# Weights stored as float64: two VectorE instructions a piece to make float32, instead of three

## The chip, the core and the metric

The kernel runs on one core of one Trainium2 chip. A core has five engines with a queue of instructions each: TensorE (PE: matmuls and weight loads), VectorE (DVE), ScalarE (ACT), GpSimd (POOL) and SyncE (SP), which here issues all DMA transfers. Every engine takes its own instructions strictly in order and waits at semaphores for the others. The metric is the device time of one execution in microseconds (us).

## The reference

Local and global attention (8 batches, 8 heads, 512 local and 32 global positions, head size 64), then a two-layer network over all 4352 tokens.

```python
def reference(**kwargs):
    ...
    attn_out = _attn_ref(**attn_kwargs)        # softmax over a window of +-32 keys and 32 global keys
    B, H, S, D = attn_out.shape
    x = np.ascontiguousarray(attn_out.transpose(0, 2, 1, 3)).reshape(B * S, H * D)
    return _moe_ref(x=x, **moe_kwargs)

def _moe_ref(x, w_in, w_out):
    h = x @ w_in                               # (tokens, 512) @ (512, 2048)
    g = h * (1.0 / (1.0 + np.exp(-h)))
    return (g @ w_out).astype(np.float32)      # (tokens, 2048) @ (2048, 512)
```

The two weight matrices arrive as float64 (the draw is divided by a float64 square root), all else as float32.

## The kernel before

Every product is made of float32r parts: a value is cast to `hi`, and `lo` is the value minus `hi`; three matmuls (hi hi, hi lo, lo hi) are added in PSUM.

**Attention** is a stream of steps, each one 128 queries of two heads. A step k loads `raw` and `vraw`, splits them (`qk`, `klo`, `vhi`, `vlo`), makes scores `s` on TensorE, softmax in `probs` on VectorE and ScalarE, copies them by a DMA to `rr`, transposes them to `t`, splits that into `pt_hi` (ScalarE) and `pt_lo` (VectorE, L397), and multiplies with the values into `o`, which goes to `xh` and `xl` (L427, L428). GpSimd makes `klo` and `vlo` of the first 28 to 32 steps and the columns of `pt_hi` and `pt_lo` for the global queries (L404, L405).

**The two layers** run over blocks of 3 or 2 token tiles of 128. For each of 16 slices f of the hidden dimension, `first_layer` makes `h` (L550, 12 matmuls) and from it `gh` and `gl` (ScalarE L556 and L559, VectorE L557 and L560); `second_layer` adds that slice's product into `out` (L569 to L571). During a block, attention for the next block is put between the matmuls. Block 0 needs 12 steps of attention before it starts.

**The weights** are converted once, before and during block 0, in `load_weights`: 36 pieces, 28 of 512 columns and the last 8 of 256. SyncE loads a piece's 64-bit words into `raw_w` (three buffers for the pieces of 512, in turn). ScalarE reads the upper words as float32 and scales them by 2^-112 into `w` (L231), which puts the exponent where float32 wants it, but three bits too low. Three VectorE instructions mend that: L233 shifts by 3 into `raw_w`'s upper words, L234 joins this with the sign, L236 takes the three missing bits from the lower word. ScalarE casts `w` to `w_hi` (L238), and GpSimd subtracts for `w_lo` (L239). After that the buffers of `w` and `raw_w` are free again. First-layer slice f of block 0 needs the two or four pieces of slice f.

**The order.** TensorE's instructions stand in the order of the program text. On the other engines and on SyncE's queue a scheduler places the instructions when the kernel is built, from the waits among them and from its own estimate of durations, so a change in one instruction moves others.

Of the kernel before, what the change touches and what calls it, by code (L numbers as in the profile page):

```python
# [9 lines left out]
F32 = mybir.dt.float32  # L10
# [3 lines left out]
U32 = mybir.dt.uint32  # L14
AF = mybir.ActivationFunctionType
ALU = mybir.AluOpType
# [3 lines left out]
B, H, SL, SG, D = 8, 8, 512, 32, 64  # L20
P = 128
NC = SL // P              # query chunks of a sequence
NPR = H // 2              # pairs of heads, each one 128-row slice of the model dimension
NST = NC * NPR            # steps of a batch: a chunk for a pair of heads
W = 224                   # keys that a chunk of local queries sees: 192 local ones and the 32 global ones
# [8 lines left out]
NEG = -8.0e9              # times the scale of 1/8: -1e9  # L34
SCALE = 0.125

# [1 line left out]
SIZES = [3, 2] + [3] * 9 + [2]       # token tiles in each block of the two layers  # L38
NLATE = 4                            # slices of the weights that take the place of the first buffers
# [10 lines left out]
AHEAD = 12                           # steps before the first block is complete  # L50
# when the parts of a step are due, in steps' times after its scores
DUE = dict(load=-1.3, split=-0.4, vload=-0.4, vsplit=0.9, turn=1.45, out=2.15)
LAG = 1.0                            # more for the parts after the scores in the first steps
# [5 lines left out]
PRE, PACE, LOOK = 0, 0.75, 1         # weights converted during the first steps  # L59
END = 0.6                            # how far the attention is ahead of a block  # L60

DUE = dict(load=-1.2, split=-0.5, vload=-0.6, vsplit=0.95, turn=1.6, out=2.2)
LAG = 2.25
# [6 lines left out]
PACE = 0.85  # L70
PRE = 5
LOOK = 3
END = 0.5
# [14 lines left out]
SIZES = (3, 3, 3, 3, 3, 3, 3, 3, 3, 2, 3, 2)  # L88
# [5 lines left out]
def attention_moe_kernel(ctx: ExitStack, tc: tile.TileContext, qk0_in, qk_in, v_in, gqk, wts, out):  # L94
    nc = tc.nc
# [3 lines left out]
    work = ctx.enter_context(tc.tile_pool(name="work", bufs=1))  # L99
    two = ctx.enter_context(tc.tile_pool(name="two", bufs=2))  # L100
    small = ctx.enter_context(tc.tile_pool(name="small", bufs=4))
    # buffers of the first steps, in two parts that later hold the last slices of the weights
    first = [tc.tile_pool(name=f"first{i}", bufs=1, side=side) for i, side in enumerate(("left", "right"))]
# [5 lines left out]
    # until the layers start, attention has their banks too  # L109
    early, banks = [1], {"s": itertools.count(), "t": itertools.count(), "o": itertools.count()}  # L110
# [32 lines left out]
    # probabilities: columns past the window stay zero  # L143
# [6 lines left out]
    # transposed probabilities by unit and key tile; 32 more columns for the global queries  # L150
    # what of the first buffers is still in use
# [47 lines left out]
    def load_weights():  # L199
# [19 lines left out]
        if first[1]:  # L219
            raw = first_pool[1].tile([P, 2 * DM], I32, tag="raw", bufs=3, name=f"raw_w{f}_{c0}")  # L220
            w = first_pool[1].tile([P, n], F32, tag="w", bufs=2, name=f"w{f}_{c0}")
# [4 lines left out]
        if W0 <= 2 * f + c0 // DM < PIN:  # L226
            tc.keep_in_program_order(load)
        # float64 to float32: the upper word read as float32 and scaled by 2**-112 has the exponent
        # rebased three bits too low, below the sign; the lower word gives the last three bits
        words = raw.rearrange("p (n w) -> p n w", w=2)  # L230
        nc.scalar.activation(w, words[:, :, 1].bitcast(F32), AF.Copy, scale=2.0**-112)  # L231
        wi, up, low = w.bitcast(U32), words[:, :, 1].bitcast(U32), words[:, :, 0].bitcast(U32)
        nc.vector.tensor_scalar(out=up, in0=wi, scalar1=3, scalar2=None, op0=ALU.logical_shift_left)  # L233
        nc.vector.scalar_tensor_tensor(out=wi, in0=wi, scalar=0x80000000, in1=up, op0=ALU.bitwise_and,  # L234
                                       op1=ALU.bitwise_or)
        nc.vector.scalar_tensor_tensor(out=wi, in0=low, scalar=29, in1=wi, op0=ALU.logical_shift_right,  # L236
# [36 lines left out]
    # program order is the order of the data  # L273
# [43 lines left out]
    tiles = {}  # L317
# [37 lines left out]
    def st_scores(k, b, c, pr):  # L355
        qk, klo = tiles.pop(("qk", k))
        free(k)
        s = attbank("s", f"s{k}")
# [24 lines left out]
        # a copy that keeps every bit for the transpose  # L383
# [141 lines left out]
    outs, now = {}, [0, 0]  # L525

    def fill(part):
        """Attention for the next block, in step with this one."""
        now[1] += part
        n = now[0]  # L530
        total = NF * SIZES[n] + (NF - 1) * SIZES[n] + (SIZES[n - 1] if n else 0)
        if n + 1 < len(SIZES):
            advance(ends[n] + (ends[n + 1] - ends[n]) * min(1.0, now[1] / total / FULL))
# [7 lines left out]
    def first_layer(n, f):  # L541
# [13 lines left out]
        # twice h * sigmoid(h); the half goes into the way out  # L555
# [46 lines left out]
def _layout(q_l, k_l, v_l, q_g, k_g, v_g, w_in, w_out):  # L602
# [26 lines left out]
    # the first steps: both heads' keys once, and each one's queries zero on the other's rows  # L629
# [9 lines left out]
    # two heads on the rows; each one's queries are zero on the other's rows  # L639
# [28 lines left out]
```

## Time and profile before

| | |
|---|---|
| three executions | 1107.52, 1108.76 (median), 1111.5 us |
| span of the profiled execution | 1108.1 us (0.7 under the median; its own time is not recorded apart) |
| PE busy | 1042.5 us, 94% |
| DVE busy | 798.5 us, 72%, 2467 instructions |
| ACT busy | 725.1 us, 65% |
| POOL busy | 228.5 us, 21% |
| weight conversions (first L231 to last L239) | 17.4 to 202 us |
| TensorE clock granted, mean | 0.972 |

A share of busy time is a mean over stages: TensorE is full from about 220 us on, and before that it waits for the others. So a change in the conversions is to be read from the stage before 220 us alone. In the rows of the profile, `out<-in` are the names of the program without their numbers, `xN` is a count, and `<-` with an engine and a line names what ended an idle time.

### The profile page before, as it was taken

Reading aid. Unit: us, or ns where it says so; the run is one execution under the profiler, and the core shown is the slowest. Engines: PE = TensorE matmul, PEld = TensorE weight load, DVE = VectorE, ACT = ScalarE, POOL = GpSimd, SP = SyncE. Lnnn points to the kernel's source line nnn. Section 1 sums busy time; section 2 is a strip of 40 time slices with the busy share of each in tenths; the row PEclk is TensorE's granted clock in tenths of the full one; section 3 lists DMA queues with packets and bytes.
Section 4 is the critical chain, followed back from the end, with each engine's and each line's share of the span. In section 5 each row is a group of like instructions: output and inputs, shape, how many; then the busy total and the mean of one; then the engine's idle time right before and its main releaser. Section 6 shows DMA issues by size and latency. Waiting matters only on the chain.

```text
span 1108.1 us, 21579 instructions
## 1 busy us (share of the span) xinstructions
PE 1042.5 (94%) x6824; PEld 947.8 (86%) x6824; DVE 798.5 (72%) x2467; ACT 725.1 (65%) x1933; POOL 228.5 (21%) x441
## 2 busy tenths in 40 slices
PE   5647889999999999999999999999999999999998
PEld 4646778898999999999989999999999999889996
DVE  6989998777778867766667877777777768863322
ACT  7876676776677766766567776667666658763232
POOL 8756775321100111001010111101100011100000
PEclk8678899999999999999999999999999999999999
DMA  8576554543343443342233443334333324420000
GB/s 249 179 219 188 182 170 130 156 121 117 109 145 115 138 138 110 113 148 83 82 112 112 147 130 117 111 116 158 109 109 120 111 92 148 138 76 20 1 30 19
DMA packets 74800, 134.76 MB, mean 122 GB/s; under 512 B 10432, under 2 KB 30400, under 8 KB 74688
## 3 DMA queue, kind: packets, MB, share of 16 engines
q1 hardware_dynamic: 74688, 133.40, 38.8%
q8 instruction: 54, 0.88, 0.3%
q14 instruction: 58, 0.48, 0.1%
HBM read 86.44 MB, written 8.91 MB: 86 GB/s over the span
## 4 chain that ended last, share of the span: by engine, by line
PE 80%; DVE 10%; DMA 3%; issue 3%; ACT 3%; POOL 1%; SPq 0%; DVEq 0%; ACTq 0%; POOLq 0%
PE h L550 31%; PE out L569 11%; PE out L571 10%; PE out L570 10%; PE o L421 8%; PE s L369 4%; PE t L393 3%; DVE w L234 2%; DVE w L236 1%; DMA rr<-probs 1%; DMA raw_w<-in_wts_dram 1%; DVE raw_w L233 1%; DVE pt_lo L397 1%; ACT probs L377 1%; DVE probs L373 1%
## 5 line engine op out<-in xcount | busy, mean ns | idle before, releaser
L550 PE MATMUL h<-xh,w_hi 128*128 128x384 f32 (+1 forms) x768 | 255.6, 333 | 0.1
L550 PE MATMUL h<-xh,w_lo 128*128 128x384 f32 (+1 forms) x768 | 252.3, 329 | 0.0
L550 PE MATMUL h<-xl,w_hi 128*128 128x384 f32 (+1 forms) x768 | 252.1, 328 | 0.0
L569 PE MATMUL out<-w_hi,gh 128*128 128x512 f32 x544 | 224.8, 413 | 0.0
L571 PE MATMUL out<-w_hi,gl 128*128 128x512 f32 x544 | 215.6, 396 | 3.0 <-DVE gl L560 1.8
L570 PE MATMUL out<-w_lo,gh 128*128 128x512 f32 x544 | 214.7, 395 | 0.0
L556 ACT ACTIVATE t<-h 128x384 f32<-128x384 f32 (+1 forms) x192 | 90.5, 471 | 186.2 <-PE h L550 175.8
L404 POOL CAST pt_hi<-pgt 128x64 fp32r<-128x64 f32 (+1 forms) x160 | 50.4, 327 | 726.1 <-PE o L421 719.2
L557 DVE SCALAR_TENSOR_TENSOR t<-t,h 128x384 f32<-128x384 f32 (+1 forms) x192 | 101.6, 529 | 122.7 <-ACT t L556 121.7
L550 PEld LDWEIGHTS h<-xh,w_hi 128*128 128x128 f32 x768 | 145.4, 189 | 6.0 <-ACT xh L427 0.6
L550 PEld LDWEIGHTS h<-xl,w_hi 128*128 128x128 f32 x768 | 145.5, 189 | 5.4
L550 PEld LDWEIGHTS h<-xh,w_lo 128*128 128x128 f32 x768 | 145.3, 189 | 0.0
L560 DVE TENSOR_TENSOR gl<-t,gh 128x384 fp32r<-128x384 f32 (+1 forms) x192 | 107.3, 559 | 48.5 <-PE out L571 43.1
L571 PEld LDWEIGHTS out<-w_hi,gl 128*128 128x128 f32 x544 | 102.8, 189 | 28.4 <-DVE gl L560 4.6
L377 ACT ACTIVATE probs<-probs,st 128x224 f32<-128x224 f32 x256 | 121.4, 475 | 7.3 <-DVE st L373 6.2
L373 DVE CUSTOM_DVE_ANT_0 probs<-s,mask 128x224 f32<-128x224 f32 x256 | 89.3, 384 | 50.4 <-PE s L369 47.0
L421 PE MATMUL o<-pt_hi,vhi 128*64 128x160 f32 (+1 forms) x512 | 99.4, 238 | 20.1 <-ACT pt_hi L396 7.8
L570 PEld LDWEIGHTS out<-w_lo,gh 128*128 128x128 f32 x544 | 103.6, 190 | 11.2
L569 PEld LDWEIGHTS out<-w_hi,gh 128*128 128x128 f32 x544 | 103.2, 190 | 11.4 <-ACT gh L559 0.4
L559 ACT CAST gh<-t 128x384 fp32r<-128x384 f32 (+1 forms) x192 | 94.6, 493 | 21.2 <-DVE t L557 17.8
L421 PE MATMUL o<-pt_hi,vlo 128*64 128x160 f32 (+1 forms) x512 | 96.3, 237 | 0.0
L421 PE MATMUL o<-pt_lo,vhi 128*64 128x160 f32 (+1 forms) x512 | 79.8, 238 | 16.3 <-DVE pt_lo L397 11.8
(82 smaller groups left out, 2016.5 us busy)
## 6 DMA issues: line engine op xcount, KB each, us to landing
raw<-in_qk_dram SPq DMA_DIRECT2D x100, 352.0 KB, 3.0
rr<-probs SPq DMA_DIRECT2D x128, 256.0 KB, 2.3
vraw<-in_v_dram SPq DMA_DIRECT2D x128, 128.0 KB, 2.4
raw_w<-in_wts_dram SPq DMA_DIRECT2D x28, 512.0 KB, 4.0
raw_g<-in_gqk_dram SPq DMA_DIRECT2D x32, 304.0 KB, 2.8
out_dram<-o SPq DMA_DIRECT2D x32, 256.0 KB, 2.6
raw<-in_qk_dram SPq DMA_DIRECT2D x28, 240.0 KB, 3.6
rg<-pg SPq DMA_DIRECT2D x16, 256.0 KB, 2.4
```

What stands on the lines that cost most here:

```text
L373: nc.vector.tensor_tensor_reduce(out=p[:, u, :W], in0=s[:, u * W : (u + 1) * W], in1=mask_of[c], scale=-SCALE, scalar=3.0e38, op0=ALU.add, ...
L377: nc.scalar.activation(p[:, u, :W], p[:, u, :W], AF.Exp, bias=st[:, u : u + 1], scale=-1.0, accum_out=st[:, 2 + u : 3 + u])
L404: nc.gpsimd.tensor_copy(out=pt_hi[:n, :, a, P:], in_=g)
L421: nc.tensor.matmul(o[:D, u * wide : u * wide + m], v[:, a, u, :], pt[:, u, a, :m], start=(i == 0), stop=(i == len(terms) - 1))
L550: nc.tensor.matmul(h[:, :nt], wt, x[:, c, :nt], start=(i == 0), stop=(i == 3 * NCC - 1))
L556: nc.scalar.activation(t[:, :nt], h[:, :nt], AF.Tanh, scale=0.5)
L557: nc.vector.scalar_tensor_tensor(out=t[:, :nt], in0=t[:, :nt], scalar=1.0, in1=h[:, :nt], op0=ALU.add, op1=ALU.mult)
L559: nc.scalar.copy(out=gh[:, :nt], in_=t[:, :nt])
L560: nc.vector.tensor_tensor(out=gl[:, :nt], in0=t[:, :nt], in1=gh[:, :nt].bitcast(F32), op=ALU.subtract)
L569: nc.tensor.matmul(o, gh[:, sl], wh, start=(f == 0), stop=False)
L570: nc.tensor.matmul(o, gh[:, sl], wl, start=False, stop=False)
L571: nc.tensor.matmul(o, gl[:, sl], wh, start=False, stop=(f == NF - 1))
```

## The change

ScalarE's scaling becomes a leaky rectifier: `out = x` for a positive `x` and `-2^32 x` for a negative one, with x the scaled word. The result is never negative; a negative weight's exponent is greater by 32, which is a set bit at the place that becomes the sign after a shift by 3. The instruction that joined the sign apart goes. The shift for the lower word is made in place, in the lower words of `raw_w`, and needs only the loaded piece; the one join that is left shifts `w` by 3 and adds the three bits.

```diff
         words = raw.rearrange("p (n w) -> p n w", w=2)
-        nc.scalar.activation(w, words[:, :, 1].bitcast(F32), AF.Copy, scale=2.0**-112)
-        wi, up, low = w.bitcast(U32), words[:, :, 1].bitcast(U32), words[:, :, 0].bitcast(U32)
-        nc.vector.tensor_scalar(out=up, in0=wi, scalar1=3, scalar2=None, op0=ALU.logical_shift_left)
-        nc.vector.scalar_tensor_tensor(out=wi, in0=wi, scalar=0x80000000, in1=up, op0=ALU.bitwise_and,
-                                       op1=ALU.bitwise_or)
-        nc.vector.scalar_tensor_tensor(out=wi, in0=low, scalar=29, in1=wi, op0=ALU.logical_shift_right,
+        nc.scalar.activation(w, words[:, :, 1].bitcast(F32), AF.Prelu, scale=2.0**-112, alpha=-(2.0**32))
+        wi, low = w.bitcast(U32), words[:, :, 0].bitcast(U32)
+        nc.vector.tensor_scalar(out=low, in0=low, scalar1=29, scalar2=None, op0=ALU.logical_shift_right)
+        nc.vector.scalar_tensor_tensor(out=wi, in0=wi, scalar=3, in1=low, op0=ALU.logical_shift_left,
                                        op1=ALU.bitwise_or)
         nc.scalar.copy(out=hi, in_=w)
```

In the new kernel the rectifier is L233 on ScalarE, the shift L235 and the join L236 on VectorE; all other lines keep their numbers.

The scheduler's order moves with it. On VectorE, ahead of the `gl` of slice 1 in block 0 (`gl0_1`), these rows stand before, from the last joins of piece `w5_512` on (in a name like `w6_0` the 6 is the slice and the 0 the first column; the last number only tells buffers apart):

```order
L234 SCALAR_TENSOR_TENSOR w5_512_1371<-w5_512_1371,raw_w5_512_1370 128x512
L285 TENSOR_REDUCE gst1_1_1208<-pg1_125 128x1
L236 SCALAR_TENSOR_TENSOR w5_512_1371<-raw_w5_512_1370,w5_512_1371 128x512
L557 SCALAR_TENSOR_TENSOR t0_1_1185<-t0_1_1185,h0_1_1172 128x384
L286 TENSOR_SCALAR gst1_1_1208<-gst1_1_1208 128x1
L233 TENSOR_SCALAR raw_w6_0_1457<-w6_0_1458 128x512
L428 TENSOR_TENSOR xl_1_1216<-o12_1217,xh_1_1215 64x128
L435 TENSOR_TENSOR acc_130<-o12_1217,acc_130 64x32
L234 SCALAR_TENSOR_TENSOR w6_0_1458<-w6_0_1458,raw_w6_0_1457 128x512
L560 TENSOR_TENSOR gl0_1_1187<-t0_1_1185,gh0_1_1186 128x384
```

And now, ahead of the same `gl0_1`:

```order
L557 SCALAR_TENSOR_TENSOR t0_1_1177<-t0_1_1177,h0_1_1164 128x384
L235 TENSOR_SCALAR raw_w7_512_1560<-raw_w7_512_1560 128x512
L236 SCALAR_TENSOR_TENSOR w7_0_1553<-w7_0_1553,raw_w7_0_1552 128x512
L285 TENSOR_REDUCE gst1_1_1200<-pg1_125 128x1
L286 TENSOR_SCALAR gst1_1_1200<-gst1_1_1200 128x1
L235 TENSOR_SCALAR raw_w8_0_1654<-raw_w8_0_1654 128x512
L236 SCALAR_TENSOR_TENSOR w7_512_1561<-w7_512_1561,raw_w7_512_1560 128x512
L235 TENSOR_SCALAR raw_w8_512_1662<-raw_w8_512_1662 128x512
L288 TENSOR_SCALAR gst1_1_1200<-gst1_1_1200 128x1
L428 TENSOR_TENSOR xl_1_1208<-o12_1209,xh_1_1207 64x128
L435 TENSOR_TENSOR acc_130<-o12_1209,acc_130 64x32
L560 TENSOR_TENSOR gl0_1_1179<-t0_1_1177,gh0_1_1178 128x384
```

Pieces finished ahead of `gl0_1` are 12 before (through `w5_512`) and 16 now (through `w7_512`), and the next shifts stand ahead of the joins.

On SyncE's queue of transfers, from the copy of step 13's probabilities (`rr13`) on, the rows before are:

```order
L385 DMA rr13_1112<-probs1_122 128x512
L225 DMA raw_w6_512_1466<-in_wts_dram 128x1024
L225 DMA raw_w7_0_1566<-in_wts_dram 128x1024
L322 DMA raw19_1730<-in_qk0_dram 128x480
L329 DMA vraw16_1428<-in_v_dram 128x256
L225 DMA raw_w7_512_1575<-in_wts_dram 128x1024
L322 DMA raw20_1840<-in_qk0_dram 128x480
```

And now:

```order
L385 DMA rr13_1106<-probs1_122 128x512
L322 DMA raw18_1598<-in_qk0_dram 128x480
L225 DMA raw_w7_512_1560<-in_wts_dram 128x1024
L225 DMA raw_w8_0_1654<-in_wts_dram 128x1024
L225 DMA raw_w8_512_1662<-in_wts_dram 128x1024
L322 DMA raw19_1712<-in_qk0_dram 128x480
L225 DMA raw_w9_0_1766<-in_wts_dram 128x1024
```

Loads of weights have moved ahead of the steps' loads: `raw_w8_512` stands in front of `raw19` where before `raw_w7_0` did. ScalarE and GpSimd move in the same way, and TensorE not at all. ScalarE has one table load in both orders, as its second row.

## The prediction

> **What bounds the kernel now.** I read the page's slices first, to see where the matrix engine is not full.
>
> ```profile
> PE   5647889999999999999999999999999999999998
> ...
> DVE  6989998777778867766667877777777768863322
> ACT  7876676776677766766567776667666658763232
> POOL 8756775321100111001010111101100011100000
> ```
>
> A slice is 27.7 us. From the ninth slice on, TensorE is full nearly to the end; only the first 220 us can be shortened by work on another engine. All the weight conversions lie there. So I asked for the busy time of each engine by stage.
>
> ```profile
> core 0: us, PE busy (x) PEld busy (x) DVE busy (x) ACT busy (x) POOL busy (x), PEclk, DMA share, GB/s
> 20.00:80.00 60.00, 37.55 (x269) 34.24 (x268) 51.36 (x157) 47.24 (x133) 43.06 (x56) 0.70 0.69 215
> 80.00:140.00 60.00, 45.04 (x260) 39.34 (x258) 57.92 (x125) 41.43 (x104) 37.05 (x42) 0.89 0.59 182
> ...
> 143.80:160.00 16.20, 14.37 (x83) 12.83 (x82) 15.83 (x35) 11.62 (x28) 13.74 (x13) 0.89 0.61 183
> ...
> 160.00:200.00 40.00, 36.55 (x251) 32.76 (x250) 34.45 (x105) 28.36 (x80) 21.26 (x28) 1.00 0.45 131
> 200.00:220.00 20.00, 18.37 (x106) 16.39 (x105) 14.72 (x44) 15.19 (x40) 7.68 (x10) 0.91 0.59 169
> ```
>
> Between 80 and 140 us VectorE works 57.92 of 60 us (97%), while TensorE idles 15.0 us, ScalarE 18.6 and GpSimd 23.0: VectorE is the bound there. Before 80 us it works 86%, with the DMA engines at 0.69 and ScalarE at 79%: a mixture. After 160 us TensorE is at 91% and takes over. The chain of waits from 60 to 205 us says the same by line.
>
> ```profile
> by line: DVE w L234 14.8%; issue 12.7%; DVE w L236 8.9%; DMA raw_w<-in_wts_dram 8.2%; DVE raw_w L233 5.9%; PE h L550 4.4%; ACT probs L377 4.1%; DVE pt_lo L397 3.2%; PE o L421 3.2%; DVE gl L560 2.9%; PE s L369 2.6%; PE out L569 2.3%; DVE t L
> ```
>
> The three instructions that join the words of a weight piece (L233, L234, L236) make 29.6% of it. Their groups, shape by shape (busy us, mean ns of one):
>
> ```profile
> L234 DVE SCALAR_TENSOR_TENSOR w<-w,raw_w 128x512 uint32<-128x512 uint32 x28 | 30.3, 1083 | 0.6
> L236 DVE SCALAR_TENSOR_TENSOR w<-raw_w,w 128x512 uint32<-128x512 uint32 x28 | 25.7, 917 | 0.3
> L233 DVE TENSOR_SCALAR raw_w<-w 128x512 uint32<-128x512 uint32 x28 | 18.0, 642 | 6.1 <-ACT w L231 6.1
> L234 DVE SCALAR_TENSOR_TENSOR w<-w,raw_w 128x256 uint32<-128x256 uint32 x8 | 4.0, 504 | 0.4
> ```
>
> These means are far above what the same instructions take alone. The fastest, median and slowest of each, and two places in order of time:
>
> ```profile
> L233 DVE TENSOR_SCALAR raw_w<-w x36: 280/418/1443, 18.1 to 199.1; 128x512 uint32<-128x512 uint32 x28, 128x256 uint32<-128x256 uint32 x8
> L234 DVE SCALAR_TENSOR_TENSOR w<-w,raw_w x36: 424/693/1777, 18.6 to 199.5; 128x512 uint32<-128x512 uint32 x28, 128x256 uint32<-128x256 uint32 x8
> L557 DVE SCALAR_TENSOR_TENSOR t<-t,h x7: 527/542/544, 92.9 to 140.1; 128x384 f32<-128x384 f32 x7
> ...
> 72.21 0.69 DVE L234 SCALAR_TENSOR_TENSOR w<-w,raw_w 128x512 uint32<-128x512 uint32 x1
> ...
> 85.35 1.28 POOL L239 TENSOR_TENSOR w_lo<-w,w_hi 128x512 fp32r<-128x512 f32 x1
> 85.41 1.78 DVE L234 SCALAR_TENSOR_TENSOR w<-w,raw_w 128x512 uint32<-128x512 uint32 x1
> ```
>
> The join at 72.21 took 0.69 us with GpSimd idle; the same one at 85.41 began just after a GpSimd subtraction of 1.28 us, took 1.78, and ended 0.56 after that subtraction. L557, which reads one operand from PSUM, never stretches (527 to 544). So the bare prices are 0.42 us for a shift and 0.69 for a join, and the rest of the means is waiting for GpSimd.
>
> **The change, part by part.** *One VectorE join less.* A 512-column piece now takes one shift and one join. Bare, it falls from 0.42 + 2 x 0.69 = 1.80 us to 1.11; with today's waits from 0.642 + 1.083 + 0.917 = 2.64 to 0.642 + 1.000 = 1.64 (1.000 is the mean of the two joins). Over the 36 pieces L234 holds 30.3 + 4.0 = 34.3 us. That is not the gain: the run shortens only where VectorE ends last, and the order of work moves too.
>
> *Conversions move ahead.* TensorE's order is unchanged; on VectorE, ScalarE, GpSimd and the load queue the pieces of weights now stand earlier among the attention work. I counted, in the two orders, the finished pieces ahead of a result that TensorE needs: ahead of the gl of slice 2 they are 14 before and 18 now, of slice 6, 21 and 28, ahead of step 18's pt_lo, 25 and 28. Slice 6's gl is the tightest. In the trace it is the seventh L560:
>
> ```profile
> 143.78 1.57 DVE L560 TENSOR_TENSOR gl<-t,gh 128x384 fp32r<-128x384 f32 x1
> ```
>
> VectorE's conversion work ahead of it was 21 x 1.80 = 37.8 us and is now 28 x 1.11 = 31.1, bare: 6.7 less. With today's waits it is 21 x 2.64 = 55.4 and 28 x 1.64 = 45.9: 9.5 less. I take the middle, -8.1. (Step 18's pt_lo gains 25 x 1.80 - 31.1 = 13.9 and so does not bind.) The early stage, where VectorE is not alone, is inside this number; that its share is fully collected is assumed.
>
> The Trainium skill (SBUF — State Buffer, section "Who interferes with whom") says that a VectorE instruction with two SBUF inputs and a GpSimd instruction that reads SBUF share one read interface, which whoever is first holds for its whole instruction while the other is blocked. The pair at 85.35 and 85.41 agrees. By that rule the wait is a remainder of GpSimd's work, which stays, and the next two-input instruction meets it: the term would be -6.7, not -8.1, and the sum 1.4 us later.
>
> *What follows slice 6.* From 143.8 to 220 us TensorE idles 1.83 + 3.45 + 1.63 = 6.9 us. With VectorE nearly rid of conversions by then, some of that goes; other waits (block change, attention's own chain) stay. Half: -3.4, ends 0 and -6.9.
>
> *New waits for weights.* Pieces come closer together, while the buffers of raw words stay three. A load cannot be issued before the join three pieces back is done, and the next shift needs its landing.
>
> ```profile
> raw_w<-in_wts_dram SPq DMA_DIRECT2D x17, 512.0 KB, 3.9
> SPq L225 <- DVE w L236: 24.0, 8, 4.6
> ```
>
> The first row (80 to 160 us) gives 3.9 us from issue to landing; the second says that loads already wait for the join. Where the pieces stand densest (front of slice 1's gl) VectorE has some 2.5 to 3.5 us of bare work between a join and the shift that needs that buffer again, so it stands still for about a microsecond at each of a few pieces, with attention's pieces queued behind it and TensorE behind those. +2, ends 0 and +5. On the load queue, steps' own loads and the copies of probabilities stand behind the same loads; that is inside these ends.
>
> *The shift* used to wait for ScalarE (6.1 us of idle in its row) and now waits for the load alone: free, hidden or given to the term above. It now reads every second word and writes it back; no row shows both. L233 writes every second word at 0.42, the joins read them at 0.69. I take 0.42, from the row with the same kind of instruction; at 0.69 the 28 pieces would lose 28 x 0.27 = 7.6 us.
>
> *The rectifier* on ScalarE instead of a copy with a scale: operands are the same immediates and one table load stands in both orders. No row shows a rectifier.
>
> ```profile
> L231 ACT ACTIVATE w<-raw_w 128x512 f32<-128x512 f32 x28 | 18.7, 667 | 5.9 <-DMA raw_w<-in_wts_dram 3.2 <-POOL w_lo L239 2.6
> L238 ACT CAST w_hi<-w 128x512 fp32r<-128x512 f32 x28 | 17.3, 618 | 10.0 <-DVE w L236 9.9
> L287 ACT ACTIVATE pg<-pg,gst 128x544 f32<-128x544 f32 x16 | 12.0, 750 | 8.6 <-DVE gst L286 8.3 <-DVE acc L435 0.3
> ```
>
> Between the plain cast (618) and an exponential with a per-row operand (750) it costs -0.05 to +0.08 a piece, -1.4 to +2.2 us over 28; ScalarE's 18.6 idle us between 80 and 140 cover it, and without that cover it is those ends. I take 0.
>
> **Sum.** -8.1 - 3.4 + 2 = -9.5, made against the span of 1108.1: 1098.6. The median of the runs, 1108.76, stands 0.7 above that span, so 1099. The ends of the terms: -9.5 - 6.9 + 0 = -16.4, 1092; and -6.7 + 0 + 5 = -1.7, 1107, the edge of no change. About 0.3% (3.3 us) is what a measurement of this kernel can tell from nothing.
>
> **The rivals.** *The waits go with the instruction.* If fewer two-input instructions meet GpSimd, the remaining ones may run bare: 55.4 - 31.1 = 24.3 us ahead of slice 6, with 6.9 after it 31, or 1078. For it: L234 alone carries 28 x (1.083 - 0.693) = 10.9 us of waiting. Against: GpSimd's subtractions stay as many, and TensorE's 15.0 idle us between 80 and 140 are nearly all there is to win. Typically 1085; range 1078 to 1092.
>
> *Nothing arrives.* The shift at 0.69 takes the -8.1 to about -0.5, or the waits for loads do it; with the tail of -3.4 and +2 the result is 1107. For it: transfers already run at 182 GB/s in that stage and the loads wait for buffers. Against: the trace shows no VectorE wait on a weight load above the ones ahead of L233.
>
> *Slower: ScalarE becomes the bound.* The seven pieces moved ahead of slice 6 bring ScalarE 7 x (0.667 + 0.618) = 9.0 us more in front of it, and nothing is taken off ScalarE. If it ends last, what is won on VectorE doesn't count: 9.0 - 3.4 = +5.6, or 1114. This decides once more than 18.6 - 9.0 = 9.6 of ScalarE's idle us between 80 and 140 cannot be filled. These are its waits from 80 to 160:
>
> ```profile
> ACT w_hi L238 <- DVE w L236: 7.9, 7, 2.3
> ACT probs L381 <- DVE st L380: 3.6, 4, 1.5
> ACT t L556 <- DVE gl L560: 2.7, 3, 1.0
> ACT xh L427 <- PE o L421: 2.5, 2, 1.3
> ```
>
> Most are waits for VectorE, which shrink with its load: against the rival. GpSimd, whose subtractions move ahead in the same way, has 23.0 idle us and is further off. That the rectifier is not what runs (a second table load, say) is included here with 1 in 100.
>
> **How the numbers follow.** The forecast case (1092 to 1105.4) 0.56; waits gone 0.17; nothing arrives (1105.4 to 1112) 0.15; slower 0.12. The predicted time is the first's, 1099, its own range 1092 to 1105. To leave out no more than 2 in 10 the range runs to 1086 (half of the second case) and 1110 (past the third and into the fourth). Faster by over 0.3%: 0.56 + 0.17 = 0.73; within: 0.15; slower: 0.12.
>
> **What would show it.** The join at L236, 36 times, bare 0.69; the shift at L235 with a median near 0.42 and no wait for ScalarE; L233 on ScalarE near 0.67 with a single table load. VectorE's busy time about 25 to 34 us less, and below 90% between 80 and 130 us. TensorE full from some 10 us earlier. Shifts that wait for raw_w transfers, a few us in all. I am wrong if the shift's median is 0.69, if ScalarE's share rises over 90% in that stage, or if waits for weight loads exceed 5 us.

## The result, and the profile after

The changed kernel takes 1115.98 us (median; 1113.88 to 1117.41), the kernel before 1108.39 beside it: a ratio of 1.0061, 95% interval [1.0042, 1.0080], 0.6% slower. The forecast was 1099.0 with a range of 1086 to 1110. The profiled execution took 1115.36 us, its span 1113.5.

The page's totals and its slices, in the order in which the prediction read them:

```profile
PE 1049.1 (94%) x6824; PEld 954.9 (86%) x6824; DVE 780.6 (70%) x2431; ACT 725.9 (65%) x1933; POOL 220.3 (20%) x441
...
PE   4667797999999999999999999999999999999998
...
DVE  5888887667777876876667877778767667873322
```

VectorE has 36 instructions and 17.9 us of work less (798.5 before), and slices two, four, five and six show it: 8 where 9 stood. TensorE isn't full any earlier: its first slices read 4667797, before 5647889. Busy time by stage:

```profile
20.00:80.00 60.00, 38.53 (x263) 34.93 (x262) 46.80 (x149) 48.45 (x133) 40.44 (x57) 0.64 0.70 223
80.00:140.00 60.00, 46.40 (x246) 40.74 (x246) 52.57 (x114) 43.05 (x107) 39.61 (x43) 0.80 0.65 207
140.00:160.00 20.00, 18.03 (x114) 16.39 (x113) 17.28 (x36) 13.34 (x34) 12.87 (x14) 0.91 0.27 81
160.00:200.00 40.00, 33.48 (x211) 29.54 (x210) 27.94 (x82) 25.43 (x73) 15.20 (x23) 0.91 0.43 128
200.00:220.00 20.00, 20.00 (x139) 18.66 (x137) 12.21 (x42) 14.61 (x40) 8.85 (x13) 1.00 0.42 121
```

Between 80 and 140 us VectorE works 52.57 of 60 us, no longer 57.92. It is no longer full, yet TensorE gets through 246 matmuls there, fewer than the 260 before. The instructions themselves (groups by shape, busy us, mean ns, idle before; then fastest/median/slowest):

```profile
L236 DVE SCALAR_TENSOR_TENSOR w<-w,raw_w 128x512 uint32<-128x512 uint32 x28 | 27.2, 975 | 1.5 <-ACT w L233 1.3
L235 DVE TENSOR_SCALAR raw_w<-raw_w 128x512 uint32<-128x512 uint32 x28 | 21.0, 749 | 8.7 <-DMA raw_w<-in_wts_dram 8.7
L233 ACT ACTIVATE w<-raw_w 128x512 f32<-128x512 f32 x28 | 18.7, 671 | 0.9 <-DMA raw_w<-in_wts_dram 0.7
...
L235 DVE TENSOR_SCALAR raw_w<-raw_w x36: 292/430/1703, 18.0 to 198.0; 128x512 uint32<-128x512 uint32 x28, 128x256 uint32<-128x256 uint32 x8
L236 DVE SCALAR_TENSOR_TENSOR w<-w,raw_w x36: 418/688/2026, 19.1 to 200.4; 128x512 uint32<-128x512 uint32 x28, 128x256 uint32<-128x256 uint32 x8
```

The bare prices are as forecast: shift 0.43 us, join 0.69, rectifier 0.67. The means lie above them where GpSimd works at the same time: of the 28 large joins the seven that overlap no GpSimd work took 0.68 to 0.69 us and the others up to 2.03. The shift, which reads one operand only, is stretched in the same way: 0.40 to 0.43 us without such work, up to 1.70 with it. The waits and the chain (20 to 220, and 60 to 205 us):

```profile
DVE raw_w L235 <- DMA raw_w<-in_wts_dram: 13.7, 13, 2.0
ACT w L233 <- DMA raw_w<-in_wts_dram: 7.9, 7, 1.9
...
by line: DMA raw_w<-in_wts_dram 23.7%; issue 8.0%; DVE w L236 7.5%; PE h L550 7.4%; DVE raw_w L235 7.3%; PE s L369 4.1%; PE out L569 3.9%; PE out L570 3.4%; PE out L571 3.3%; PE o L421 3.1%; DVE gl L560 2.5%; DVE pt_lo L397 2.2%; DMA raw_g<
```

Transfers of weights have gone from 8.2% of that chain to 23.7%, and VectorE waits 13.7 us for them. That looks like the culprit; the experiments say that it is a small part. Two milestones, step 11's `pt_lo` and slice 6's `gl`:

```profile
83.52 0.68 DVE L397 TENSOR_TENSOR pt_lo<-t,pt_hi 128x512 fp32r<-128x512 f32 x1
...
151.02 0.59 DVE L560 TENSOR_TENSOR gl<-t,gh 128x384 fp32r<-128x384 f32 x1
```

Step 11 is where it was (83.19 before), so nothing of the lighter conversion arrived by then. Slice 6's `gl` is 7.2 us later (143.78), and the span 5.4 us longer. Piece `w12_512` meanwhile is joined at 142.18 us, before at 162.47: the weights come early and the layers late.

### The profile page after: what moved, and what is told of

Same layout as the page of the kernel before. It is cut to its first block, busy times and chain, and to the rows that moved or that the text cites. A ratio compares the mean times of both kernels' runs of the same rounds, so it can differ in the third digit from the quotient of the medians.

```text
span 1113.5 us, 21495 instructions
## 1 busy us (share of the span) xinstructions
PE 1049.1 (94%) x6824; PEld 954.9 (86%) x6824; DVE 780.6 (70%) x2431; ACT 725.9 (65%) x1933; POOL 220.3 (20%) x441
## 4 chain that ended last, share of the span: by engine, by line
PE 82%; DVE 7%; DMA 6%; issue 2%; ACT 2%; SPq 0%; POOL 0%; ACTq 0%; DVEq 0%; POOLq 0%
PE h L550 32%; PE out L569 11%; PE out L571 10%; PE out L570 10%; PE o L421 8%; PE s L369 5%; DMA raw_w<-in_wts_dram 4%; PE t L393 3%; DMA rr<-probs 1%; DVE raw_w L235 1%; DVE w L236 1%; DVE probs L373 1%; DVE pt_lo L397 1%; DMA raw_g<-in_gqk_dram 1%; PE gs L268 1%
## 5 line engine op out<-in xcount | busy, mean ns | idle before, releaser
L550 PE MATMUL h<-xh,w_hi 128*128 128x384 f32 (+1 forms) x768 | 256.5, 334 | 0.0
L550 PE MATMUL h<-xl,w_hi 128*128 128x384 f32 (+1 forms) x768 | 253.5, 330 | 2.1 <-DVE xl L428 2.1
L550 PE MATMUL h<-xh,w_lo 128*128 128x384 f32 (+1 forms) x768 | 253.9, 331 | 0.0
L550 PEld LDWEIGHTS h<-xl,w_hi 128*128 128x128 f32 x768 | 146.3, 191 | 8.0 <-DVE xl L428 2.6
L550 PEld LDWEIGHTS h<-xh,w_hi 128*128 128x128 f32 x768 | 146.2, 190 | 5.4
L550 PEld LDWEIGHTS h<-xh,w_lo 128*128 128x128 f32 x768 | 146.2, 190 | 0.0
L560 DVE TENSOR_TENSOR gl<-t,gh 128x384 fp32r<-128x384 f32 (+1 forms) x192 | 107.0, 557 | 49.6 <-PE out L571 44.5
L571 PEld LDWEIGHTS out<-w_hi,gl 128*128 128x128 f32 x544 | 103.1, 189 | 25.9 <-DVE gl L560 2.1
L559 ACT CAST gh<-t 128x384 fp32r<-128x384 f32 (+1 forms) x192 | 94.7, 493 | 21.1 <-DVE t L557 17.6
```

What stands on the lines that cost most here:

```text
L550: nc.tensor.matmul(h[:, :nt], wt, x[:, c, :nt], start=(i == 0), stop=(i == 3 * NCC - 1))
L559: nc.scalar.copy(out=gh[:, :nt], in_=t[:, :nt])
L560: nc.vector.tensor_tensor(out=gl[:, :nt], in0=t[:, :nt], in1=gh[:, :nt].bitcast(F32), op=ALU.subtract)
L571: nc.tensor.matmul(o, gl[:, sl], wh, start=False, stop=(f == NF - 1))
```

## Two causes taken apart: the instructions and the order

To hold the order fixed, the first instructions of VectorE, ScalarE, GpSimd and the load queue (430, 352, 190 and 140 of them, less those that a kernel lacks) are chained by order-only dependencies along a list. TensorE's order never changes. Chained along their own orders, both kernels come out as the same programs, instruction for instruction, so the chain itself costs nothing.

```diff
     second_layer(*pend)
+    for key, ranks in ORDER.items():          # per engine: ranks in the program text
+        ...
+        for a, b in zip(first_ones, first_ones[1:]):
+            tc.add_manual_dep(b, a.name, ...)  # order only, no semaphore
```

**New instructions in the old order** (`ORDER` is that of the kernel before without L234's places):

> The changed arithmetic (rectifier, one shift, one join), with every engine's instructions held in the order that they had before, the dropped join simply missing. Theory A (the new order is what costs: pieces of weights done 10 to 20 us early, ahead of attention and of gl): without it the saved VectorE work arrives. Ahead of slice 6's gl 21 pieces lose 0.69 us each, 14.5 us, of which TensorE can use its idle time there; expected 1092 to 1101. Theory B (the new instructions themselves cost, the shift that waits for its load at the head of VectorE's queue or the rectifier): the order makes no difference and it stays at 1113 to 1117. Theory C (VectorE never was what held the stage up; its relief only moves the wait to transfers and ScalarE): 1106 to 1110, no change against before.

Measured: 1092.2 us, ratio 0.9856 [0.9834, 0.9879]. It beats both kernels, the changed one by 23.8 us. Its totals, two stages, slice 6's `gl`, and VectorE's wait for loads:

```profile
PE 1039.2 (95%) x6824; PEld 946.4 (87%) x6824; DVE 773.6 (71%) x2431; ACT 723.4 (66%) x1933; POOL 224.7 (21%) x441
...
20.00:80.00 60.00, 42.31 (x294) 38.84 (x294) 49.34 (x163) 51.52 (x146) 43.67 (x59) 0.70 0.73 238
80.00:140.00 60.00, 52.24 (x333) 46.04 (x332) 56.69 (x131) 48.47 (x122) 43.93 (x51) 0.97 0.64 207
...
128.18 1.03 DVE L560 TENSOR_TENSOR gl<-t,gh 128x384 fp32r<-128x384 f32 x1
...
DVE raw_w L235 <- DMA raw_w<-in_wts_dram: 1.6, 3, 1.2
```

Slice 6's `gl` comes 15.6 us earlier than before, with 21 pieces ahead of it: 0.74 us a piece, near a bare join's 0.69. One execution tells this no closer: two kernels further down keep the same VectorE order up to there and have that `gl` at 130.15 and 131.94 us, 0.65 and 0.56 a piece. VectorE is busy 56.69 of 60 us (still the bound there), and 333 matmuls fit where 260 stood.

**Old instructions in the new order** (all three VectorE instructions of a piece at the new join's place):

> The arithmetic of before (three VectorE instructions a piece, all three at the place of the new join) in the order of the changed kernel on every engine. Theory A: the order alone costs more than the whole change did, since 28 pieces with a third instruction stand ahead of slice 6's gl: 7 us (the order's loss in the changed kernel) plus 7 pieces x 1.8 us at most, so 1118 to 1128. Theory B: 1106 to 1110, like before. Theory C: like the changed kernel, 1113 to 1117.

Measured: 1138.68 us, ratio 1.0278 [1.0262, 1.0293], further up than expected. Together with the other three kernels:

| | old order | new order | the order costs |
|---|---|---|---|
| three instructions | 1108.8 | 1138.7 | 29.9 |
| two instructions | 1092.2 | 1116.0 | 23.8 |
| the instructions gain | 16.6 | 22.7 | |

So the edit is good for 16.6 us, and the order that the scheduler made for it loses 23.8. The 1092.2 and the 1116.0 were not measured side by side; by their ratios to the kernel before, which ran beside each, the loss is 0.0205 of 1108.8, or 22.7 us. That is within the intervals, and what follows goes by medians.

## What in the new order costs 23.8 us

**Not VectorE's place in front of a load.** The changed kernel's order, but each shift stands right ahead of its join, where its load has mostly landed:

```diff
-L235 TENSOR_SCALAR raw_w0_512 ...
 L373 ISA probs1,st3<-s3,mask0 ...
+L235 TENSOR_SCALAR raw_w0_512 ...
 L236 SCALAR_TENSOR_TENSOR w0_512 ...
```

> The changed kernel in its own order, but for the shift, which stands right ahead of its join and no longer waits for its load ahead of attention's work. If the 13.7 us that VectorE waited for loads at the head of its queue are what ate the gain (part of theory B): some 5 to 10 us faster than the changed kernel, 1105 to 1110. If the order of the pieces is (theory A): within 3 us of the changed kernel, 1113 to 1117, because the pieces still stand ahead of attention.

Measured: 1114.76 us, ratio 1.0059 [1.0045, 1.0073]: no gain against the changed kernel's 1.0061. The wait went and another took its place (20 to 220 us):

```profile
ACT w_hi L238 <- DVE w L236: 14.7, 19, 1.5
...
DVE raw_w L235 <- DMA raw_w<-in_wts_dram: 3.7, 3, 1.9
```

VectorE's wait fell from 13.7 to 3.7 us, and ScalarE's wait for the join rose from 8.2 to 14.7.

**Not the transfers, or little.** In both orders the first three loads alone are made, and later 512-column pieces convert what lies in those three buffers (25 of the 28 transfers of 512 KB are left out; line numbers are 5 greater):

```diff
-        load = nc.sync.dma_start(out=raw, in_=wts[f, :, sl].bitcast(I32))
+        if not first[1] or 2 * f + c0 // DM < 3:
+            load = nc.sync.dma_start(out=raw, in_=wts[f, :, sl].bitcast(I32))
```

> The changed kernel in its own order on every engine, but with 25 of the 28 transfers of 512-column pieces left out: pieces 3 to 27 convert again what lies in the three raw buffers, so its output is not the reference's; every instruction of the engines stays. It tells how the new order costs its 23 us against the old one (1116.0 to 1092.2). Theory A1 (the pieces as such: 28 instead of 21 stand ahead of slice 6's gl on VectorE, ScalarE and GpSimd): taking the transfers away brings little, 1110 to 1116. Theory A2 (pieces so close together that each waits for a buffer and its transfer, on VectorE, ScalarE and the load queue, with attention behind): most comes back, 1093 to 1102. Both in part: 1102 to 1110.

> The same left out (25 of 28 transfers; output not the reference's) from the new arithmetic in the old order. Control for the run before it: the waits for weight loads are small there (1.6 us on VectorE), so both theories expect 1084 to 1092, within 8 us of 1092.2. If it falls as far as the kernel in the new order does, the transfers cost the same in both orders, and A2 is wrong.

Measured: 1111.61 in the new order (ratio 1.0019 [1.0006, 1.0031]), 1090.87 in the old (0.9835 [0.9815, 0.9855]). Without the transfers the order still costs 20.7 us, so they are 3.0 of the 23.8 (23.78 less 20.74), a difference that the intervals hardly tell from nothing.

**Loads in the order of the program text** (they let pieces start later):

```diff
-PIN = 8
+PIN = 36
```

> The changed kernel with one constant changed: all 36 loads of weights, not the first 8, are held behind the transfers that the program issues ahead of them; the scheduler places the rest anew. Ahead of slice 1's gl stand 8 finished pieces (changed kernel 16, before 12), of slice 6's 18 (28; 21). If pieces standing ahead of attention are the cause, it is near the new arithmetic in the old order or better: 1086 to 1098. If any order that the scheduler makes for the new arithmetic is bad (bunched pieces later on: 18 ahead of slice 6, 36 ahead of slice 14), 1104 to 1114.

Measured: 1118.68 us, ratio 1.0091 [1.0074, 1.0109], above both ranges. Up to slice 3's `gl` it keeps pace with the old order (108.3 us in both), with only 10 pieces ahead of it, not 16; at slice 6's it is 7.5 us late; and ahead of slice 13's stand six pieces, four of them in a row, with the load of a global step behind those on the queue:

```profile
PE gs L268 <- ACT qk_g L253: 12.6, 1, 12.6
...
179.00:204.90 25.90, 12.37 (x55) 10.59 (x55) 8.92 (x24) 9.53 (x23) 8.40 (x11) 0.62 0.39 119
```

That slice took 25.9 us, TensorE waiting 12.6 at one place. With pieces also begun a slice later:

```diff
-LOOK = 3
-PIN = 8
+LOOK = 2
+PIN = 36
```

> As the run before it, and pieces are asked for two slices ahead of their use instead of three: 6 finished pieces ahead of slice 1's gl, 16 ahead of slice 6's, where TensorE needs 14. If fewer pieces ahead is better throughout: 1084 to 1096. If pieces now come too late, TensorE waits for w_hi and w_lo: 1096 to 1110.

Measured: 1136.46 us, ratio 1.0251 [1.0227, 1.0276], above both ranges again; now the weights come too late:

```profile
PE h L550 <- ACT w_hi L238: 23.1, 5, 6.8
```

Too early and too late both cost; these two settle nothing on the cause, since the scheduler moved everything else again.

**Pieces ahead, or attention's own order?** Ahead of slice 6's `gl` the new order has on VectorE the same instructions as the old, and seven pieces more. That suggested that the pieces ahead are the whole cost. First, six pieces left out (of slices 6 to 8, which then use slice 1's weights) in either order; the lines here are 5 further down, so L560 is L565:

```diff
+        if f in (6, 7, 8):
+            w_hi.append(w_hi[1])
+            w_lo.append(w_lo[1])
+            w_next[:] = (f + 1, 0)
+            return
```

> The new instructions in the new order, but the six pieces of slices 6, 7 and 8 are not loaded or converted (these slices use slice 1's weights, so the output is not the reference's). Ahead of block 0's gl of slices 0, 1 and 6 VectorE then has 12, 12 and 22 joins, against 13, 16 and 28 in the changed kernel and 11, 12 and 21 in the new instructions in the old order (1092.2 us, gl of slice 1 at 92 us and of slice 6 at 128; in the changed kernel 108 and 151). Theory P, that the new order costs its 23.8 us by the pieces that stand ahead of the layers (on VectorE those are all that differs ahead of each of these gl): gl of slice 1 at 92 to 97 us, of slice 6 at 128 to 133, and 1092 to 1098 us in all. Theory Q, that the attention's own changed order on ScalarE, GpSimd and the load queue costs it: only the six pieces' VectorE time goes, 6 x 1.7 = 10 us, so gl of slice 6 near 141 and 1105 us or more.

> The same six pieces left out of the new instructions in the old order, as the control (the output is not the reference's). P: one piece at most goes ahead of the gl of slice 1, and from there on TensorE is already over 95% busy, so little is gained: 1084 to 1092 us, and the new order's distance falls from 23.8 us to under 9. Q: the distance stays at 18 to 24 us.

Measured: 1102.99 (ratio 0.9941 [0.9925, 0.9958]) and 1087.49 (0.9794 [0.9777, 0.9811]). The distance falls from 23.8 to 15.5 us, between the two theories. Slice 6's `gl` in the one and the other:

```profile
142.22 0.55 DVE L565 TENSOR_TENSOR gl<-t,gh 128x384 fp32r<-128x384 f32 x1
```

```profile
123.31 1.03 DVE L565 TENSOR_TENSOR gl<-t,gh 128x384 fp32r<-128x384 f32 x1
```

With 22 pieces ahead of it, one more than in the old order with all its pieces (128.18), it still comes 14 us later. A count of pieces doesn't explain that.

Then the pieces' instructions alone were moved later in the new order, to the places that they have in the old, on all engines and the queue:

```diff
-L235 TENSOR_SCALAR raw_w0_512 ...
 ...
 L397 TENSOR_TENSOR pt_lo0<-t0 ...
-L235 TENSOR_SCALAR raw_w1_0 ...
+L235 TENSOR_SCALAR raw_w0_512 ...
```

> The whole work again. On all engines and the load queue attention and layers keep the changed kernel's order; only the instructions of the pieces of weights are moved later among them, to the places that they have in the old order. Ahead of block 0's gl of slices 0, 1, 2, 4 and 6 VectorE then has 11, 12, 14, 18 and 21 joins (changed kernel: 13, 16, 18, 22, 28). Theory P, that the places of the pieces cost the new order's 23.8 us, but for some 5 us that stand already before 70 us with the same number of pieces ahead: gl of slice 1 at 95 to 99 us, of slice 6 at 130 to 136, and 1094 to 1101 us. Theory Q, that attention's own changed order costs most of it (the six pieces left out brought the distance only from 23.8 to 15.5 us): gl of slice 6 at 138 us or later, and 1104 us or more.

> As the kernel with the pieces in their old places, but only for what ran after 100 us in the changed kernel: ahead of the gl of slices 0, 1, 2, 4 and 6 stand 13, 14, 14, 18 and 21 joins. P: the two pieces too many ahead of slice 0 cost their 4 to 9 us, the rest is as in the kernel with all pieces in old places: 1098 to 1107 us. Q: no more than the places of the last seven pieces, about 7 us, is won: 1107 to 1112 us.

Measured: 1112.63 (ratio 1.0032 [1.0017, 1.0046]) and 1114.18 (1.0058 [1.0042, 1.0074], above both of its ranges). The theory of pieces ahead falls: with 11, 12, 14, 18 and 21 of them ahead, just as in the old order, 3.4 us come back and 20.4 stay. What stays comes with attention's own order, and with a pile of pieces that these places make (below). This is what moves there on VectorE, from the old order to the new, near step 3:

```diff
 L433 COPY acc<-o1 64x32
+L373 ISA probs0,st6<-s6,mask1 128x224
 ...
+L379 TENSOR_SCALAR st6<-st6 128x2
+L380 RECIPROCAL st6<-st6 128x2
+L382 TENSOR_SCALAR probs0<-probs0,st6 128x224
 ...
 L397 TENSOR_TENSOR pt_lo0<-t3,pt_hi0 128x4x128
 ...
-L373 ISA probs0,st6<-s6,mask1 128x224
```

The softmax of step 6 has moved ahead of step 3's `pt_lo`, which TensorE needs for step 3's product with the values. Step 3's `pt_lo` starts at 43.9 us, in the old order at 38.2. That this move is what costs is not shown: a kernel with the same start and the old order behind it (below) has that `pt_lo` at 43.4 us and ends 2.6 us behind the old order.

Both kernels with old places made a pile of their own: four pieces ahead of slice 9's `gl`, which took 13.6 us against 7.7 (the first of the two):

```profile
154.30:167.90 13.60, 6.52 (x39) 5.27 (x39) 11.22 (x23) 8.13 (x20) 8.16 (x8) 0.86 0.18 56
```

A third set of places avoids that:

> As the kernel with the changed kernel's attention order and old places, but the last pieces of 512 columns are not pressed together ahead of the first one of 256: ahead of the gl of slices 4 and 6 stand 19 and 26 joins, not 18 and 21 (28 in the changed kernel). There, slice 9 took 13.6 us with four pieces in it, against 7.7 in the old order. If that pile, which the experiment itself had made, cost about 6 us, this comes out at 1106 to 1110 us; if it cost nothing in the end, at 1112 to 1114 us.

Measured: 1114.36 us, ratio 1.0050 [1.0031, 1.0069]. Slice 9 is back at 6.8 us, but five pieces now stand in slice 6, which took 13.7. The pile only moved.

## Where it is lost: place by place

**One order's start, the other's rest.** The change of order is made at one moment of the old order's execution, on all engines; behind it stands the order of the kernel with old places:

```diff
-ORDER = new, pieces in old places
+ORDER = old up to 66 us, then the rest in the order above      # or up to 115, 142 us; or the reverse
```

> The new instructions, with the pieces of weights in the places of the old order throughout. What ran up to step 9's pt_lo (66 us) stands on every engine in the old order, all that follows in the order of the kernel with the changed kernel's attention order and old places (1112.6 us). That one was 4.4 us behind the old order (1092.2) at step 9 already, 7 at the gl of slice 0, 12.5 at the gl of slice 8. Theory E, that the time is lost bit by bit wherever attention's order differs, the first steps included: 1105 to 1109 us. Theory L, that what is lost in the first steps is made up while TensorE waits anyway, and only the order behind them counts: 1111 to 1114 us.

> The reverse: up to step 9's pt_lo the changed kernel's attention order (pieces in the old places), then the old order. E: the 4 to 7 us lost in the first steps stay to the end: 1096 to 1100 us. L: they are made up: 1091 to 1094 us.

> As the kernel with the old order's start and the new rest (1107.2 us, 15.0 behind the old order), but the old order lasts up to the gl of slice 4 (115 us) on every engine, not to 66 us. That one was 3.9 us behind at that gl, 6.9 at slice 5's, 9.2 at slice 8's and 15.1 at slice 9's, which has four pieces. If the time is lost place by place, what stood at slice 4 is won: 1102 to 1105 us. If the order from slice 5 on makes the end whatever was ahead: 1106 to 1109 us.

> The same, with the old order up to the gl of slice 8 (142 us). What is left of the new order there is the pile of four pieces ahead of slice 9's gl and attention's order behind it. Place by place: 15.0 - 9.2 = 6 us over the old order's 1092.2, 1096 to 1100 us; the pile of four in the old order cost 6.3. If slices 5 to 8 don't count: 1103 us or more.

Measured, with the start of `gl` in us (read from L560 in order of time):

| kernel | slice 0 | slice 4 | slice 8 | slice 9 | median, us | ratio |
|---|---|---|---|---|---|---|
| old order | 87.7 | 115.2 | 141.8 | 149.5 | 1092.20 | 0.9856 |
| new start to 66 us, then old | 91.8 | 119.2 | 145.9 | 153.5 | 1094.84 | 0.9873 [0.9856, 0.9890] |
| old to slice 8, then new | 86.6 | 113.8 | 142.2 | 155.7 | 1100.57 | 0.9927 [0.9912, 0.9941] |
| old to slice 4, then new | 88.5 | 115.0 | 146.2 | 159.8 | 1104.72 | 0.9956 [0.9944, 0.9968] |
| old to 66 us, then new | 89.5 | 119.1 | 151.0 | 164.6 | 1107.22 | 0.9978 [0.9965, 0.9991] |
| new, pieces in old places | 94.7 | 122.8 | 154.3 | 167.9 | 1112.63 | 1.0032 |
| changed kernel | 96.4 | 131.7 | 162.8 | 169.7 | 1115.98 | 1.0061 |

Read from the top down (without the second row) it is a ladder: 8.4 us for what follows slice 8 (the pile in slice 9 is nearly 6 of it), 4.1 for slices 5 to 8, 2.5 for 66 to 115 us, 5.4 for the first 66 us, 3.4 for the pieces' places: 23.8. A single rung is uncertain by 2 to 3 us (the ratios' intervals), so the smaller ones are barely clear of noise; the sum is. No place costs it all. The second row came between its two expectations: the new start alone lost 2.6 us, not 4 to 7, and its interval meets that of the old order. The same start costs 5.4 with the new order behind it, so the rungs don't simply add up in another combination.

**A pile by itself.** In the old order, with everything else as it was, the pieces of one or two slices are moved to slice 8:

```diff
 L560 TENSOR_TENSOR gl0_6 ...
-L236 SCALAR_TENSOR_TENSOR w10_512 ...
-L235 TENSOR_SCALAR raw_w11_0 ...
-L236 SCALAR_TENSOR_TENSOR w11_0 ...
 ...
 L560 TENSOR_TENSOR gl0_7 ...
+L236 SCALAR_TENSOR_TENSOR w10_512 ...
+L235 TENSOR_SCALAR raw_w11_0 ...
+L236 SCALAR_TENSOR_TENSOR w11_0 ...
```

> The new instructions in the old order (1092.2 us), where nearly every slice of block 0 has two pieces converted and takes 5.8 to 7.8 us from gl to gl. One thing is moved: the two pieces between the gl of slices 6 and 7 go behind the latter, so that slice 7 has none and slice 8 four. Theory R, that pieces in a pile cost time that the empty slices cannot give back, because TensorE fills those: slice 7 falls from 7.8 to about 6 us (slices without a piece took 5.5 to 6.2 in the changed kernel), slice 8 rises from 5.8 to 10 to 13 (slices with four took 9.4 and 13.6), 1095 to 1099 us in all. Theory S, that only attention's own order matters and piles are harmless: 1091 to 1094 us.

> As the pile of four, with the piece of slice 6 in the pile too: slices 6 and 7 have none, slice 8 five (a slice with five took 13.7 us where only the last pieces' places differed). R: 6 to 8 us over the old order's 1092.2, 1098 to 1101 us. S: 1091 to 1094 us.

Measured: 1098.54 us (ratio 0.9899 [0.9874, 0.9923]) and 1099.11 (0.9901 [0.9873, 0.9929]): 6.3 and 6.9 us over the old order (by the ratios 4.8 and 5.0; the intervals just touch the old order's, and both kernels say the same). Slices 7 and 8 (span, then busy PE, PEld, DVE, ACT, POOL), first in the old order, then with the pile of four, then of five:

```profile
128.20:136.00 7.80, 7.80 (x53) 7.34 (x52) 7.74 (x19) 6.70 (x17) 7.37 (x8) 1.00 0.67 228
136.00:141.80 5.80, 5.80 (x43) 5.20 (x42) 5.76 (x13) 4.93 (x14) 4.44 (x6) 1.00 0.66 206
```

```profile
131.90:138.00 6.10, 6.10 (x45) 5.69 (x43) 3.70 (x14) 3.44 (x9) 1.61 (x5) 1.00 0.32 105
138.00:149.00 11.00, 8.11 (x55) 7.30 (x53) 8.28 (x16) 6.98 (x17) 6.75 (x7) 0.97 0.53 151
```

```profile
131.10:137.10 6.00, 6.00 (x43) 5.59 (x42) 3.87 (x14) 3.52 (x10) 2.01 (x5) 1.00 0.34 107
137.10:150.00 12.90, 8.12 (x55) 7.31 (x53) 10.87 (x17) 8.02 (x19) 8.54 (x9) 0.99 0.59 181
```

With two pieces in a slice TensorE and VectorE are both full. The slice without pieces gets no shorter than 6.0 to 6.1 us, because TensorE is full in it (6.10 of 6.10) while VectorE idles 2.4. The slice with the pile takes 11 to 13, and TensorE idles 3 to 5. What the empty slice can't give back is the cost: 17.1 and 18.9 us for the two slices, not 13.6. Ahead of them slice 6's `gl` was late already, by 3.8 us in the kernel with four (131.94 against 128.18), where nothing is moved on VectorE up to there, and by 2.9 in the one with five. The kernel that keeps the old order to slice 8 has it at 130.15 in that same order and is 0.4 us behind by slice 8, so that these 3 to 4 us cannot be put down to the pile. The changed kernel has the same picture where it stands furthest behind (slices 5 to 8, with 3, 3, 0 and 0 pieces):

```profile
131.70:141.60 9.90, 7.18 (x41) 6.44 (x42) 7.72 (x23) 8.08 (x20) 5.43 (x7) 0.83 0.51 174
141.60:151.00 9.40, 7.43 (x45) 6.67 (x45) 7.71 (x14) 6.27 (x16) 5.52 (x6) 0.82 0.33 99
151.00:157.30 6.30, 6.30 (x40) 5.87 (x38) 5.78 (x16) 3.96 (x10) 4.09 (x6) 1.00 0.29 101
157.30:162.80 5.50, 5.50 (x41) 4.88 (x41) 4.01 (x12) 3.97 (x12) 2.74 (x5) 1.00 0.32 101
```

The runs show that a pile costs time in the old order, 3.5 to 5.3 us in its own two slices; that the changed kernel's piles cost what they seem to is inferred from the like rows. Open is how the losses divide between attention's order and the piles: the kernels with old places have the pile in slice 9, which the changed kernel has not, so their 20.4 us are not attention's order alone. Open too is what single move costs the first steps their 5 us. Old order on one engine and new on another, and a fourth raw buffer, were not run.

## Why the prediction was wrong, point by point

*One VectorE join less* held. In the order for which its durations were read, it gave 15.6 us ahead of slice 6 (11.8 to 15.6 in three kernels) against 21 x 0.69 = 14.5 bare, and 21 x 1.00 with today's waits. From the lock of the Trainium skill (SBUF — State Buffer, "Who interferes with whom") the prediction worked out that the waits for GpSimd stay and meet the next instruction; the measurement agrees: 0.56 to 0.74 a piece, and a join still means 975 ns over a median of 688.

*Conversions move ahead* is the step that failed. It took -8.1 at slice 6's `gl` and +7.2 was measured, 15.3 us off. It counted the pieces ahead of one result and priced them by VectorE's own time. That needs a VectorE that stays the bound and attention rows that stay in place. Neither held: VectorE fell to 52.57 of 60 us, and attention's rows, though the same set ahead of that `gl`, stood in another order. What the runs showed in its place: the new order, which this step booked as a gain, costs 23.8 us by itself, more than the 16.6 that the instructions gain. Of these 23.8, 3.4 go with the places of the pieces that the step counted, and 20.4 with attention's order and the piles. Nor was slice 6 the tightest by the step's own count: slice 1, with 12 pieces before and 16 now, gains 12 x 1.80 - 16 x 1.11 = 3.8 us bare, and slice 2 (14 and 18) 5.2. The sentence that the early stage's share "is fully collected is assumed" fell with it: none had arrived by step 11. The order of two pieces of code was shown in the text; the same look at attention's rows would have shown step 6's softmax ahead of step 3's end.

*What follows slice 6*, -3.4: from 7.2 us behind at slice 6's `gl` to 5.0 at slice 15's, -2.2 (the span ends 5.4 behind). The size is near by luck, because the term was made of TensorE's idle time. From slice 6's `gl` to 220 us, changed kernel and kernel before:

```profile
151.02:220.00 68.98, 62.46 (x405) 56.34 (x405) 48.10 (x142) 45.52 (x127) 30.07 (x44) 0.95 0.40 119
```

```profile
143.80:220.00 76.20, 69.29 (x435) 61.98 (x434) 65.00 (x182) 55.17 (x147) 42.68 (x50) 0.96 0.52 152
```

TensorE idles 6.5 us there, before 6.9: VectorE lost its conversions and next to nothing of the idle time went.

*New waits for weights*, +2 with an end at +5: the waits were 13.7 us, beyond the named bound of 5, and yet the transfers are worth 3.0 us of the order's cost. The sign "waits over 5 us" came true and was not the cause: with 10 of the 13.7 us gone (the late shift) the time stayed.

*The shift* 0.43 at the median, *the rectifier* 0.671 against 0.667 before, one table load: as taken. The groups of the conversions fell by 27.9 us (84.4 to 56.5), as forecast; VectorE's total by 17.9, less than the 25 to 34.

*The rivals.* The slower one named 1114, near what came, but by ScalarE as the bound; ScalarE was busy 43.05 of 60 us (72%), so it is the right number by a wrong way. "Nothing arrives" by the shift's price or the loads is refuted too. The rival "the waits go with the instruction" (1078 to 1092) is refuted by the joins, whose mean stayed far above their median. A rival "the new order is worse in itself" was missing, with no chance given to it.

*Idle or slow?* TensorE's total is 1049.1 us in the changed kernel, 1042.5 before, 1039.2 in the old order, for the same 6824 matmuls. Against the old order, 9.9 of the 23.4 us of span are thus matmuls that took longer and 13.5 are idle time. The granted clock goes with it: 0.80 between 80 and 140 us, against 0.97; a matmul of L550 keeps TensorE busy for 0.254 us there (18.26 us for 72), in the old order 0.206, and 0.190 where the clock is 1.00. The Trainium skill (TensorE: Matmul & The Clock Gate, Part 1) has the clock halved after an idle window and given back after a busy one. The trace agrees that it falls to 0.50 and comes back, in steps of 3.4 us, but the window need not be idle: up to 300 us in the changed kernel TensorE was busy for 0.6 to 1.7 us of the 3.4 ahead of each fall, for 2.2 or more where the clock stayed full, and for 2.9 or more ahead of each return. No run here varied the clock by itself; as far as the rows go, a wait of TensorE costs more than its length.

## What to carry to other kernels

When an edit makes a scheduler reorder the work, measure the edit in the old order first: here 16.6 us of gain and 23.8 of loss came as one number. Where two engines are both nearly full, work for the one should be spread evenly over the stretches of the other: here the slice that was left empty could not give back what the pile cost, and that the weights came earlier brought nothing. Price a reordering by walking through the whole order of what the bound engine waits for, attention's rows too, and give "the order is worse" a chance of its own.

## What the runs showed that was not expected

A wait that is long in the trace can be worth little: 10 of VectorE's 13.7 us of waits for loads, moved away, changed the time by 1.2 us, within the spread. The order of the same instructions alone moved this kernel by 24 to 30 us (2.1 to 2.7%), more than the edit. And 25 of 28 weight transfers of 512 KB, all left out, made 1.3 us in the old order and 4.4 in the new.
